# Attention ahead of a soft mixture of experts: softmax weights as the stationary operand, values with a column of ones as the moving one

## The chip, the cores and the metric

The kernel runs on one core of a Trainium2 chip. A core has a matrix engine (TensorE, PE in the profile; its weight loads have a row of their own, PEld), a vector engine (VectorE, DVE), a scalar engine for functions and copies (ScalarE, ACT), a general engine (GpSimd, POOL) and SyncE (SP), which here only issues DMAs. The engines run side by side, each through its own instructions in order, and wait for each other by semaphores. TensorE multiplies a stationary operand, which a weight load brings into its array, by a moving operand that is streamed past it, and writes to PSUM, a small memory of eight banks of 2 KB per partition. ScalarE and VectorE carry results from there to SBUF, the main on-chip memory; GpSimd reads and writes only SBUF.

The metric is the device time of one execution in microseconds (us).

## The reference

```
rotate(x)  = rotary embedding of q and k, by position and frequency       # batch 8, heads 8, seq 576, dim 64
scores     = rotate(q) @ rotate(k).T / sqrt(64)
attn       = exp(scores - max(scores))
attn       = attn / (sum(attn) + 1e-9)
x          = attn @ v                            # joined over heads: 4608 tokens x 512
logits     = x @ phi                             # 4608 x 32 slots
d          = softmax of logits over the tokens;  slot_input = d.T @ x
slot_out   = relu(slot_input[e] @ w1[e]) @ w2[e] # 8 experts, 4 slots each, 512 -> 1024 -> 512
c          = softmax of logits over the slots
out        = c @ slot_out                        # 4608 x 512, float32
```

Everything is float32. Only the score products are split by the kernel into float16 high and low halves.

## The kernel before

The work is cut into 32 pairs of heads (`NPAIR`): two heads of one batch, one on partitions 0 to 63 and the other on 64 to 127. Four pairs make a batch. The 576 tokens are nine blocks of 64 keys, and the queries are two halves of 288 (`HC`). Small products use TensorE's array as four quadrants of 64x64, so that four products of 64 rows and 64 columns can run at once; an entry such as `64*64 64x288` in the profile is one such product, stationary shape first, moving shape second. A float32 product takes two rows in the profile, a float16 product one.

For each pair, by the names in the code:

- `load0`, `load1` (L137) bring q and k; `spin0`, `spin1` (L142, GpSimd) multiply by cosines and sines, `join` (L146, VectorE) adds the two products, `high0`, `high1` (L151, ScalarE) and `low` (L155, VectorE) split the result into float16 halves. The loaded tile `x_in` has two buffers, and `low` is its last reader. `load_v` (L161) brings the values.
- `m00` to `m31` and `m_rem` (L175, L183) are score products of the high halves alone, and VectorE takes their maximum per query (L177, L185); `m_min`, `m_turn`, `m_half`, `m_rows` (L193, L200, L204, L209) make rows of it, which a small DMA puts into `peak`.
- `t0` to `t8` (`score`, L225) are the scores of one key block with **keys on partitions** and queries along the free axis: three float16 products and a fourth that subtracts the maxima, 16 rows in all. ScalarE takes the exponential (L226) into `a_t`, three key blocks to a buffer, three buffers.
- `av0` to `av8` (L238): the values of a key block (64 keys x 64) are stationary and the softmax weights (64 keys x 288 queries) are moving. The result `o_ps` has the value's 64 dimensions on partitions, that is, x transposed and not yet divided. There is one `o_ps`, of two banks. `o_out` (L246, ScalarE) copies it to `xt`.
- The softmax's sums are made apart: `add` (L252, VectorE) adds three key blocks to three others, `total` (L263, TensorE) multiplies by columns of ones (`pick`) so that the sums of both heads come out as rows, `total_out` (L269) copies them. `send` (L274), `recip` (L280), `spread` (L286) and `widen` (L293) carry the sums through SBUF and DRAM and back as a full tile of reciprocals by DMAs; `norm` (L297, GpSimd) multiplies `xt` by it. The last two pairs do this by products instead (`sums_turn`, `sums_wide`, `norm_wide`: L303, L317, L322).
- `natural` (L331, L332) turns the divided `xt` back by transposes of 128x128, and `natural_out` (L337, L338, ScalarE) copies it to `xn`, tokens on partitions. `logits` (L346) needs `xt`, once per batch for four pairs; the slot products of the batch (L389 to L404) need `xn`; they are done in small steps (`step0` to `step2`), with the softmax over slots (L411 to L427).

Score, maximum, sums, turning and logits products share three PSUM tiles of two banks (`ps_s`), taken in turn.

The order of each engine's instructions is written by hand. `WHEN` gives every step an offset; four units of offset are one pair, and step `s` of pair `p` stands at `WHEN[s] + 4p`. All engines' instructions, the DMA issues on SyncE among them, are issued in that order.

The experts' weights are loaded during attention into free SBUF (`weights`, `trickle0` to `trickle3`) as far as it holds them. After the last pair come a tail for that pair and the last batch (L674 to L780), the experts (L789, L813) and the combination with output DMAs (L840 to L843). In the tail `swap` (L685) and `keep` (L679) are products whose results nobody reads. `swap` uses float32 products of 64x64 stationary by 64x65 moving in the four quadrants.

```
for n in range(2):                                   # av, L235 to L239
    for h in range(2):
        r = rows[h ^ n]
        nc.tensor.matmul(o[rows[h], n, 0:HC], lhsT=vt[r, i, n], rhs=ats[p, g][r, b, half[n]],
                         start=(i == 0), stop=(i == NB - 1))
```

## Time and profile before

| | |
|---|---|
| median of 3 runs | 550.15 us (550.13 to 553.4) |
| the profiled execution's own time | 549.75 us |
| its span in the profile | 548.0 us |
| attention, first to last `o_out` (L246) | 46.3 to 473.6 us |
| busy: PE, PEld, DVE, ACT, POOL | 515.7, 389.2, 429.7, 311.6, 326.4 us |
| moved by DMAs | 111.35 MB, mean 203 GB/s |

The profile is one execution. A row of a group reads: line, engine, operation, output<-inputs, shapes, xcount, then busy time in us and mean duration of one in ns, then the idle time of the engine just before them and what ended it. A row of the timeline reads: start in us, length in us, engine, line, operation, xcount. A row of the table by stretches reads: stretch, its length, busy time and number of instructions of PE, PEld, DVE, ACT and POOL, granted TensorE clock (1.00 is full), share of the DMA engines' time, GB/s. Matmuls are pipelined, so several overlap and a row's length holds the latency of its last one.

### The profile page before, as it was taken

The page shows a single profiled execution, that of the slowest core. Times are in us where ns is not written, and L with a number is a line of the kernel's source. Part 1 is how long each engine was busy: PE and PEld are TensorE (multiplying, and loading weights), DVE is VectorE, ACT ScalarE, POOL GpSimd, SP SyncE. Part 2 cuts the span into 40 slices and gives each one's busy share as a digit, 9 for nine tenths or more (in the row PEclk, how much of TensorE's full clock was granted, in tenths as well). Part 3 has the DMA queues.
Part 4 walks back from the last instruction along what each step waited for, and adds up shares of the span by engine and source line. Part 5 has one row for each costly group of instructions (what it writes and reads, how often), then busy time and mean ns, then how long its engine had stood idle before and what let it go on. Part 6 is the DMA issues. An engine that isn't in the chain of part 4 may idle for free.

```text
span 548.0 us, 25344 instructions
## 1 busy us (share of the span) xinstructions
PE 515.7 (94%) x11325; PEld 389.2 (71%) x11325; DVE 429.7 (78%) x580; ACT 311.6 (57%) x655; POOL 326.4 (60%) x324
## 2 busy tenths in 40 slices
PE   4679999999999999999999999999999999999982
PEld 2267787877787777777887788777878886754551
DVE  5779998879998999899988998899889953232352
ACT  2146566666666666656675666566656665354441
POOL 1957787666886688668876887687678111210000
PEclk9689999999999999999999999999999999999997
DMA  7264566666566566556655665566434256459998
GB/s 263 93 216 134 193 194 193 193 192 193 194 194 193 192 192 195 190 183 202 196 195 159 220 197 195 169 204 206 138 120 121 70 182 218 169 190 411 407 417 343
DMA packets 51292, 111.35 MB, mean 203 GB/s; under 512 B 11504, under 2 KB 28656, under 8 KB 51184
## 3 DMA queue, kind: packets, MB, share of 16 engines
q1 hardware_dynamic: 51170, 109.73, 59.7%
q8 instruction: 89, 1.46, 1.1%
q14 instruction: 19, 0.16, 0.1%
q10 hardware_dynamic: 14, 0.00, 0.0%
HBM read 99.93 MB, written 9.58 MB: 200 GB/s over the span
## 4 chain that ended last, share of the span: by engine, by line
PE 87%; DVE 6%; DMA 4%; ACT 1%; issue 1%; SPq 0%; DVEq 0%; ACTq 0%
PE o_ps L238 26%; PE s_ps L225 26%; PE s_ps L263 9%; PE s_ps L175 6%; PE s_ps L331 3%; PE s_ps L789 3%; PE s_ps L346 2%; DVE nm L177 2%; DMA w_exp<-in_w 2%; PE s_ps L400 1%; PE s_ps L813 1%; PE s_ps L200 1%; DVE x_in L146 1%; DMA out<-w_exp 1%; PE s_ps L183 1%; DMA x_in<-in_qk 1%
## 5 line engine op out<-in xcount | busy, mean ns | idle before, releaser
L142 POOL TENSOR_TENSOR x_in<-x_in,cs_sb 128x288 f32<-128x288 f32 x248 | 254.5, 1063 | 80.8 <-DMA x_in<-in_qk 69.0
L226 ACT ACTIVATE a_t<-s_ps 128x576 f32<-128x576 f32 x288 | 179.6, 653 | 89.5 <-PE s_ps L225 89.2
L177 DVE TENSOR_REDUCE nm<-s_ps 128x2 f32<-128x576 f32 x256 | 183.0, 750 | 41.3 <-PE s_ps L175 39.5
L238 PE MATMUL o_ps<-a_t,v_in 64*64 64x288 f32 x2304 | 195.8, 408 | 0.0
L225 PE MATMUL s_ps<-hl 64*64 64x288 f16 x3456 | 166.5, 285 | 4.1 <-DVE nm L177 3.2
L225 PEld LDWEIGHTS <-hl 64*64 64x64 f16 x3456 | 124.6, 107 | 29.4 <-issue 6.5
L225 PE MATMUL s_ps<-peak,lift 64*64 64x288 f16 x1152 | 99.8, 284 | 0.3 <-issue 0.3
L238 PEld LDWEIGHTS o_ps<-a_t,v_in 64*64 64x64 f32 x2304 | 85.7, 133 | 8.2 <-issue 0.5
L175 PE MATMUL s_ps<-hl 64*64 64x288 f16 x1024 | 79.6, 290 | 4.1 <-DVE nm L177 4.0
L297 POOL TENSOR_TENSOR xt<-xt,rb 128x576 f32<-128x576 f32 x30 | 48.0, 1599 | 32.2 <-ACT a_t L226 13.1
L252 DVE TENSOR_TENSOR c_t<-a_t 128x1728 f32<-128x1728 f32 x32 | 62.8, 1961 | 0.0
L155 DVE TENSOR_TENSOR hl<-x_in,hl 128x1152 f16<-128x1152 f32 x32 | 60.1, 1880 | 0.5 <-ACT hl L151 0.5
L175 PEld LDWEIGHTS <-hl 64*64 64x64 f16 x1024 | 38.3, 106 | 24.7 <-issue 15.5
L146 DVE TENSOR_TENSOR x_in<-x_in 128x1152 f32<-128x1152 f32 (+2 forms) x36 | 55.3, 1535 | 0.1
L151 ACT CAST hl<-x_in 128x576 f16<-128x576 f32 (+1 forms) x66 | 40.1, 653 | 23.5 <-DVE x_in L146 21.6
L225 PEld LDWEIGHTS <-lift 64*64 64x64 f16 x1152 | 46.5, 107 | 0.7 <-issue 0.5
L337 ACT COPY xn<-s_ps 128x512 f32<-128x512 f32 x31 | 18.1, 583 | 29.1 <-PE s_ps L332 29.1
L420 POOL TENSOR_TENSOR ln<-ln,cm 128x160 f32<-128x160 f32 x7 | 14.7, 2096 | 32.4 <-DVE cm L419 32.4
L269 ACT ACTIVATE s<-s_ps,bits 128x144 f32<-128x144 f32 x32 | 12.2, 381 | 34.6 <-ACT xn L338 14.2
L263 PE MATMUL s_ps<-c_t,pick 128*32 128x144 f32 x768 | 30.4, 289 | 0.7 <-DVE c_t L252 0.5
L263 PE MATMUL s_ps<-a_t,pick 128*32 128x144 f32 x768 | 29.7, 286 | 0.0
L263 PEld LDWEIGHTS s_ps<-c_t,pick 128*32 128x32 f32 x768 | 21.1, 109 | 6.3 <-issue 4.7
(175 smaller groups left out, 463.7 us busy)
## 6 DMA issues: line engine op xcount, KB each, us to landing
x_in<-in_qk SPq DMA_DIRECT2D x62, 576.0 KB
w_exp<-in_w SPq DMA_DIRECT2D x63, 512.0 KB
v_in<-in_v SPq DMA_DIRECT2D x32, 576.0 KB
out<-w_exp SPq DMA_DIRECT2D x18, 512.0 KB
rb<-r_row SPq DMA_DIRECT2D x60, 144.0 KB
x_in<-in_qk SPq DMA_DIRECT2D x4, 288.0 KB
cs_sb<-in_cs SPq DMA_DIRECT2D x2, 288.0 KB
wk<-in_w SPq DMA_DIRECT2D x1, 512.0 KB
```

What stands on the lines that cost most here:

```text
L142: eng.tensor_tensor(out=x[:, :, c], in0=x[:, :, c], in1=cs_sb[:, :, c], op=ALU.mult)
L146: nc.vector.tensor_tensor(out=x[:, t, 0, c], in0=x[:, t, 0, c], in1=x[:, t, 1, c], op=ALU.add)
L151: nc.scalar.copy(out=halves[p][:, 1 + t, c], in_=loaded[p][:, t, 0, c])
L155: nc.vector.tensor_tensor(out=hl[:, 0:4:3], in0=x[:, :, 0], in1=hl[:, 1:3], op=ALU.subtract)
L175: nc.tensor.matmul(s[rows[c ^ h], h, 0:HC], lhsT=hl[rows[h], QH, at:at + 64], rhs=hl[rows[h], KH, half[n]], start=True, stop=True)
L177: nc.vector.tensor_reduce(out=nms[p][:, n, j:8:4], in_=s[:, :, 0:HC], axis=AX.X, op=ALU.max, negate=True)
L225: nc.tensor.matmul(s[rows[h ^ n], n, 0:HC], lhsT=lhs, rhs=rhs, start=(x == 0), stop=(x == 3))
L226: nc.scalar.activation(out=ats[p, g][:, b].rearrange("p (n x) -> p n x", n=2), in_=s[:, :, 0:HC], func=AF.Exp, scale=SCALE)
L238: nc.tensor.matmul(o[rows[h], n, 0:HC], lhsT=vt[r, i, n], rhs=ats[p, g][r, b, half[n]], start=(i == 0), stop=(i == NB - 1))
L252: nc.vector.tensor_tensor(out=c, in0=ats[p, 0], in1=ats[p, 1], op=ALU.add)
L263: nc.tensor.matmul(s[32 * k:32 * k + 32, 0, 0:QC], lhsT=pick[:, 16 * n:16 * n + NS], rhs=(c, a)[x // GRP][:, x % GRP, QC * k:QC * k + QC], ...
L297: eng.tensor_tensor(out=xts[p], in0=xts[p], in1=rbs.pop(p), op=ALU.mult)
```

## The change

The product of softmax weights and values is turned round. A block of 64 keys x 64 queries of the softmax weights is now stationary, and the values of the key block (64 keys x 65) are moving. The 65th column of the values is all ones, appended on the host before the launch, so column 65 of the result is the sum of the softmax weights of each query. Queries come out on partitions. For each key block and pair there are 5 query blocks x 2 halves x 2 heads = 20 products; the fifth query block of each half overlaps its neighbour by 32 queries, since 288 is not a multiple of 64.

With that:

- `add`, `total`, `total_out`, `send`, `spread`, `widen`, `sums_turn`, `sums_wide`, `norm_wide` and their tiles go.
- `o_out` copies 2 x 325 columns to `o_sb`, and a small piece (32 partitions) to its place. `recip` (VectorE) adds 1e-9 to ten sums per partition and takes the reciprocal; `norm` (GpSimd) multiplies by it, broadcast along 64 columns, and writes `xn` directly.
- `natural` makes `xt` from `xn`, in the other direction than before, by 18 float32 products of 64x64 with the identity, and `natural_out` copies it to `xt`.
- For the last pair `norm_last` does the division on VectorE straight from PSUM; the tail's dummy products are `keep` alone.
- `a_t` holds one key block, with five buffers, in place of three blocks and three buffers. `v_in` moves to another pool; `xn` gets a second buffer.
- All offsets in `WHEN` are new. The written start-up order becomes the table `EARLY`, with the same steps in the same order. All events of all pairs are sorted once.
- The order of output rows changes with the order of queries; the host puts them back.

```diff
-N_A = 3
+N_A = 5
 WHEN = {
...
-    -1.617, "m_half": -1.613, "m_rows": -0.965, "t0": -0.022, "weights": 0.144, "t1": 0.412, "t3": 0.469,
-    "trickle0": 0.55, "av0": 0.559, "t4": 0.734, "t5": 0.974, "t2": 1.021, "step0": 1.301, "av1": 1.367, "av3":
...
-    "trickle3": 3.55, "av6": 3.726, "send": 3.739, "av8": 4.36, "o_out": 4.366, "sums_turn": 4.847,
...
+    "load0": -14.043, "load1": -13.839, "spin0": -12.647, "spin1": -10.775, "join": -8.82, "high0": -7.86,
+    "high1": -7.28, "low": -6.571, "m01": -6.082, "m10": -5.808, "m00": -5.219, "m11": -4.394, "m21": -3.683,
+    "m20": -3.282, "m30": -3.213, "m31": -2.371, "m_rem": -1.686, "m_min": -1.251, "m_turn": -1.007, "m_half":
+    -0.955, "load_v": -0.217, "weights": 0.144, "m_rows": 0.478, "t0": 0.478, "trickle0": 0.55, "t3": 0.846,
+    "t1": 1.021, "t2": 1.273, "av0": 1.383, "t5": 1.452, "t4": 1.466, "trickle1": 1.55, "step0": 1.561, "av3":
+    1.773, "av1": 1.875, "t6": 2.093, "av4": 2.24, "t7": 2.32, "trickle2": 2.55, "t8": 2.695, "step2": 2.733,
+    "av2": 2.893, "av5": 3.27, "step1": 3.28, "av6": 3.379, "trickle3": 3.55, "av7": 4.077, "av8": 4.747,
+    "o_out": 4.753, "recip": 5.468, "norm": 6.011, "natural": 7.348, "natural_out": 7.577, "logits_late": 7.868,
+    "logits": 8.028, "logits_out": 8.396, "stats": 8.996, "logits_out_late": 9.497,
 }
...
     def load_v(p):
-        vts[p] = late.tile([P, NB, 2, 64], F32, name="v_in")
+        vts[p] = att.tile([P, NB, 2, 65], F32, name="v_in", bufs=2)
...
     def score(p, i):
-        g, b = divmod(i, GRP)
-        if b == 0:
-            ats[p, g] = att.tile([P, GRP, S], F32, name="a_t", bufs=N_A)
+        ats[p, i] = att.tile([P, S], F32, name="a_t", bufs=N_A)
...
     def av(p, i):
...
-        o, vt, (g, b) = os_[p], vts[p], divmod(i, GRP)
-        for n in range(2):
-            for h in range(2):
-                r = rows[h ^ n]
-                nc.tensor.matmul(o[rows[h], n, 0:HC], lhsT=vt[r, i, n], rhs=ats[p, g][r, b, half[n]],
-                                 start=(i == 0), stop=(i == NB - 1))
+        o, vt, at = os_[p], vts[p], ats.pop((p, i))
+        for u in range(5):
+            for n in range(2):
+                for h in range(2):
+                    r, q = rows[h ^ n], (HC * n + 64 * u if u < 4 else (256, 512)[n])
+                    nc.tensor.matmul(o[rows[n], h, 65 * u:65 * u + 65], lhsT=at[r, q:q + 64], rhs=vt[r, i, n],
+                                     start=(i == 0 and u == 0), stop=(i == NB - 1 and u == 4))
...
     def o_out(p):
-        xts[p] = late.tile([P, S], F32, name="xt", bufs=N_X)
-        nc.scalar.copy(out=xts[p].rearrange("p (n x) -> p n x", n=2), in_=os_.pop(p)[:, :, 0:HC])
...
+        osb[p] = t = att.tile([P, 2, 5, 65], F32, name="o_sb", bufs=N_O)
+        o = os_.pop(p)
+        nc.scalar.copy(out=t.rearrange("p h u x -> p h (u x)"), in_=o[:, :, 0:325])
+        nc.scalar.copy(out=t[32:64, :, 4, :], in_=o[96:128, :, 260:325])
+
+    def recip(p, src=None):
+        src = osb[p] if src is None else src
+        rrs[p] = rr = small.tile([P, 2, 5], F32, name="rr", bufs=2)
+        nc.vector.tensor_scalar_add(out=rr, in0=src[:, :, :, 64], scalar1=1e-9)
+        nc.vector.reciprocal(out=rr, in_=rr)
 
     def norm(p, eng):
-        eng.tensor_tensor(out=xts[p], in0=xts[p], in1=rbs.pop(p), op=ALU.mult)
...
+        eng.tensor_tensor(out=xn[:, :, 0:4], in0=t[:, :, 0:4, 0:64],
+                          in1=rr[:, :, 0:4].unsqueeze(3).broadcast_to([P, 2, 4, 64]), op=ALU.mult)
+        eng.tensor_tensor(out=xn[0:64, :, 4], in0=t[0:64, :, 4, 0:64],
+                          in1=rr[0:64, :, 4].unsqueeze(2).broadcast_to([64, 2, 64]), op=ALU.mult)
...
     def natural(p):
...
-        for j in range(4):
-            nc.tensor.transpose(t[:, 0, j * P:(j + 1) * P], xt[:, j * P:(j + 1) * P], id_sb)
-        nc.tensor.transpose(t[0:64, 1, 0:P], xt[:, 512:576], id_sb)
...
+        for j in range(5):
+            for r in range(2 if j < 4 else 1):
+                for c in range(2):
+                    nc.tensor.matmul(t[rows[c], r, 64 * j:64 * j + 64],
+                                     lhsT=xns[b][rows[r], j, pp * P + 64 * c:pp * P + 64 * c + 64],
+                                     rhs=id_sb[rows[r], rows[r]], start=True, stop=True)
+
+    def natural_out(p, copy=nc.scalar.copy, rest=nc.scalar.copy):
+        xts[p] = xt = late.tile([P, S], F32, name="xt", bufs=N_X)
+        t = flat.pop(("n", p))
+        copy(out=xt[:, 0:512].rearrange("p (j r x) -> p j r x", j=4, r=2),
+             in_=t[:, :, 0:256].rearrange("p r (j x) -> p j r x", j=4))
+        rest(out=xt[:, 512:S], in_=t[:, 0, 256:320])
...
-    swap(6, 64)
-    sums_turn(p)
-    swap(3, 64)
-    sums_wide(p)
-    norm_wide(p)
-    swap(6, 32)
+    norm_last(p)
+    keep(9)
+    natural(p)
+    natural_out(p, rest=nc.vector.tensor_copy)
+    keep(5)
     logits(p)
     logits_out(p, True)
-    natural(p)
-    swap(8, 64)
+    keep(9)
...
+    vl = np.concatenate([vl, np.ones_like(vl[..., :1])], axis=-1)
```

More of the change, by code (lines that the diff above doesn't have):

```diff
@@ L611, in attn_softmoe @@
             high(0, t, c)
[L612 to L616 removed]
+    done.update((n, 0) for n in ("spin0", "spin1", "join", "high0", "high1", "load0", "load1"))
+    done.add(("join", 1))
+    cold = bank2()
     heat(N_WARM)
[L619 to L622 removed]
```

250 lines of the change are left out of this document (70 added, 180 removed), and 6 rows, old and new, of tables (EARLY, WHEN).

## The prediction

> **What bounds the kernel now.** I read the page first, for the engines and the chain that ended last, then the table by stretches and the list of waits, for whether that engine ever waits in the steady stretch.
>
> ```profile
> PE 515.7 (94%) x11325; PEld 389.2 (71%) x11325; DVE 429.7 (78%) x580; ACT 311.6 (57%) x655; POOL 326.4 (60%) x324
> PE 87%; DVE 6%; DMA 4%; ACT 1%; issue 1%; SPq 0%; DVEq 0%; ACTq 0%
> 180.00:220.00 40.00, 40.00 (x964) 31.64 (x957) 37.90 (x47) 25.38 (x52) 30.74 (x29) 1.00 0.62 196
> PE s_ps L225 <- issue: 1.1, 2, 0.8
> 98.72 0.64 ACT L246 COPY xt<-o_ps 128x576 f32<-128x576 f32 x1
> 430.86 0.64 ACT L246 COPY xt<-o_ps 128x576 f32<-128x576 f32 x1
> ```
>
> TensorE (PE) carries 87% of the chain. In the stretch from 180 to 220 us it is busy for all of its 40.00 us at full clock (1.00), VectorE (DVE) for 37.90. The fourth line is all that the list of waits has for PE between 60 and 440 us. So an attention pair (two heads) costs what PE needs for it, with DVE close behind. L246 runs once per pair; between its fifth and its twenty-ninth run lie 24 pairs, so one takes (430.86 - 98.72) / 24 = 13.84 us.
>
> A busy share says little about one kind of matmul, because four 64x64 quadrants overlap. I therefore take the distance from the start of one row to the start of the next, in one steady pair:
>
> ```profile
> 204.29 0.30 PE L175 MATMUL s_ps<-hl 64*64 64x288 f16 x4
> 204.53 0.66 PE L331 MATMUL s_ps<-id_sb,xt 128*128 128x128 f32 x4
> 205.02 0.27 PE L332 MATMUL s_ps<-id_sb,xt 128*64 128x128 f32 x1
> 205.22 0.94 PE L263 MATMUL s_ps<-c_t,pick 128*32 128x144 f32 x24
> 205.98 0.92 PE L263 MATMUL s_ps<-a_t,pick 128*32 128x144 f32 x24
> 206.83 0.32 PE L175 MATMUL s_ps<-hl 64*64 64x288 f16 x4
> ...
> 208.11 0.32 PE L225 MATMUL s_ps<-peak,lift 64*64 64x288 f16 x4
> 208.23 0.32 PE L175 MATMUL s_ps<-hl 64*64 64x288 f16 x4
> 208.35 0.68 PE L238 MATMUL o_ps<-a_t,v_in 64*64 64x288 f32 x8
> 208.84 0.56 PE L225 MATMUL s_ps<-hl 64*64 64x288 f16 x12
> ```
>
> One `av` unit (L238, 8 rows: four f32 products, two rows each) holds PE for 208.84 - 208.35 = 0.49 us. The sums (L263) hold it for 206.83 - 205.22 = 1.61, the transposes of x (L331, L332) for 205.22 - 204.53 = 0.69. Four rows of L175 take 208.35 - 208.23 = 0.12 among their own kind but 0.24 ahead of L331: changing from 64x64 tiles to 128x128 costs 0.12.
>
> **The av units.** Each becomes 20 products of 64x65, 40 rows with 40 weight loads. The kernel before already holds that shape, by accident of its tail (L685 keeps PE busy there):
>
> ```profile
> L685 PE MATMUL o_ps<-acc,id_sb 64*64 64x65 f32 x136 | 2.7, 222 | 0.8 <-ACT xt L246 0.8
> 475.54 0.58 PE L685 MATMUL o_ps<-acc,id_sb 64*64 64x65 f32 x24
> 476.05 1.22 PE L317 MATMUL s_ps<-id_sb,rn 72*64 72x72 f32 x32
> 479.36 1.16 PE L685 MATMUL o_ps<-acc,id_sb 64*64 64x65 f32 x64
> ```
>
> It has the same stationary size, moving width, quadrants and banks. Taking the last row's length (0.22) from the busy time, a start follows a start by (1.16 - 0.22) / 63 = 15.0 ns; in the burst of 24 by (0.58 - 0.22) / 23 = 15.7. A new unit then takes 40 x 15.0 = 0.60 us, 0.11 more than 0.49; nine units: **+0.99 us per pair**. Bounds: if only columns counted, 61 ns per row x 65/288 = 13.8 ns (0.55 us a unit); if quadrants overlapped no better than the 72x72 products of L317, which run two at a time, (1.22 - 0.22) / 31 = 32 ns (1.28 us). I take 15.0, the row of the same shape.
>
> The Trainium skill, "TensorE: Matmul & The Clock Gate", section "Wait — 56ns, not 53.3ns?", says that starts never come closer than about 25 ns, however few columns; by that a unit would be 1.0 us and the kernel would end near 630. As a distance between starts the burst's 15.0 ns disagrees and leaves it no chance; as a pace kept up for long it is the first rival.
>
> **What PE loses.** `total` goes: **-1.61** (24 products, 48 rows). `natural` becomes 18 products of 64x64, 36 rows: 36 x 15.0 = 0.54 for 0.69, **-0.15**, and stays in 64x64 tiles, **-0.12**. Sum per pair: +0.99 - 1.61 - 0.15 - 0.12 = **-0.89 us**.
>
> **The other engines**, which must follow at 13.84 - 0.89 = 12.95 us:
>
> ```profile
> L177 DVE TENSOR_REDUCE nm<-s_ps 128x2 f32<-128x576 f32 x256 | 183.0, 750 | 41.3 <-PE s_ps L175 39.5
> L252 DVE TENSOR_TENSOR c_t<-a_t 128x1728 f32<-128x1728 f32 x32 | 62.8, 1961 | 0.0
> L155 DVE TENSOR_TENSOR hl<-x_in,hl 128x1152 f16<-128x1152 f32 x32 | 60.1, 1880 | 0.5 <-ACT hl L151 0.5
> L146 DVE TENSOR_TENSOR x_in<-x_in 128x1152 f32<-128x1152 f32 x30 | 51.1, 1705 | 0.0
> L280 DVE RECIPROCAL rr<-rc 96x12 f32<-96x12 f32 x30 | 6.4, 213 | 0.0
> L142 POOL TENSOR_TENSOR x_in<-x_in,cs_sb 128x288 f32<-128x288 f32 x248 | 254.5, 1063 | 80.8 <-DMA x_in<-in_qk 69.0
> L297 POOL TENSOR_TENSOR xt<-xt,rb 128x576 f32<-128x576 f32 x30 | 48.0, 1599 | 32.2 <-ACT a_t L226 13.1
> L427 POOL TENSOR_TENSOR cn_sb<-ln,cm 128x160 f32<-128x160 f32 x7 | 3.2, 459 | 2.6 <-DVE cm L426 2.6
> L226 ACT ACTIVATE a_t<-s_ps 128x576 f32<-128x576 f32 x288 | 179.6, 653 | 89.5 <-PE s_ps L225 89.2
> L269 ACT ACTIVATE s<-s_ps,bits 128x144 f32<-128x144 f32 x32 | 12.2, 381 | 34.6 <-ACT xn L338 14.2
> L338 ACT COPY xn<-s_ps 64x128 f32<-64x128 f32 x31 | 8.0, 258 | 0.0
> ```
>
> DVE needs nine maxima x 0.75 + 1.96 + 1.88 + 1.71 + 0.21 = 12.51 us per pair; without the 1.96 of `c_t` and with one more small operation like L280 (0.21) 10.76, so it falls further behind PE. GpSimd (POOL) multiplies 512 + 128 elements by a broadcast: at L427's 2.87 ns each 1.84 us for 1.60, and 8 x 1.06 + 1.84 = 10.3 is still under 12.95. ScalarE (ACT) copies 650 columns (0.72) and a small piece (0.26) where it copied 576 (0.64, the rows of L246 above), and drops L269 (0.38): nothing gained or lost. All are costed at nothing, because PE's 12.95 us covers them; if DVE or POOL ran short, the price would be what it exceeds that by.
>
> **Queues and buffers.** The offsets of the written order count four to a pair, so one is 3.2 us. SyncE loses `send`, `spread` and `widen` (two issues) per pair, which stood ahead of x_in loads. The maxima's rows go out on SyncE behind `load_v` and a weight load and must land before t0: from `m_half` (-0.955) to t0 (0.478) are 1.43 offsets, 4.6 us.
>
> ```profile
> 204.25 0.25 ACT L204 ACTIVATE mr<-s_ps 9x128 f16<-9x128 f32 x1
> ```
>
> Before, L204 ends at 204.50 and the rows are used at 208.11, so 3.6 us are enough: no cost. `load_v` moves from -3.19 to -0.217 and is used at 1.383 (1.6 offsets, 5.2 us later); x_in, loaded from -14.043 as soon as `low` of two pairs back has freed its buffer, is rotated from -12.647 on (1.4 offsets, 4.5 us). In the pair shown a load of that size is used 4.1 us after its issue, POOL waiting for it:
>
> ```profile
> 212.25 0.33 SPq L137 DMA_DIRECT2D x_in<-in_qk  x1
> ...
> 216.39 8.29 POOL L142 TENSOR_TENSOR x_in<-x_in,cs_sb 128x288 f32<-128x288 f32 x8 [2.15 <-DMA x_in<-in_qk]
> ```
>
> So both are in time, x_in by little; a late one costs POOL first, which has 2.6 us to spare in a pair, and PE only behind that. Nothing.
>
> A softmax buffer now holds one key block, five in all; by the order at most five are open at once (t8 of a pair waits for none that `av` has not freed), again no cost. On ACT `high1` (0.72) and the longer `o_out` (0.753) now stand ahead of the exponentials of t3, t1, t2, while PE may run only three score banks ahead: at 0.65 us per exponential and 0.48 per score unit (16 rows, L175's four being 0.12) PE may stand there for up to 0.5 us a pair. Against it stands DVE's relief, up to 0.3. I take **+0.10 per pair**.
>
> **Ends.** The last two pairs lose the sums by products: L317 above for pair 30 (1.2 us; pair 31's lies in the tail). In the tail:
>
> ```profile
> 473.63 0.64 ACT L246 COPY xt<-o_ps 128x576 f32<-128x576 f32 x1
> 478.20 0.54 PE L346 MATMUL s_ps<-xt,phi_sb 128*32 128x128 f32 x16
> L337 DVE COPY xn<-s_ps 128x512 f32<-128x512 f32 x1 | 0.7, 681 | 0.0
> ```
>
> From the last `av` to the logits 478.20 - 473.63 = 4.6 us. After: two small DVE operations (0.5), a multiply like L337 on DVE (0.68), two small ones (0.26 each, as ACT's L338), `natural` 0.54, its copy 0.6 (as L246's 0.64), handovers 0.5 (estimated): 3.3. Gain 1.3, between 0 and 2; the weight stage behind it only shifts. The start-up I leave as it is.
>
> **Sum.** 31 distances between `o_out`s x (-0.89 + 0.10) = -24.5; -1.2; -1.3: **-27.0 us**. Against the profiled run's 549.75 us (span 548.0): 522.8; the median of the runs shown is 0.4 higher: **523**.
>
> **Rivals.** *PE can't issue so densely for long (slower).* A pair would hold 360 av, 144 score, 36 maxima, 36 `natural` and some 24 other rows: 600, each with its weight load. 12.95 us ask for 21.6 ns per row throughout; the stretch above has 964 in 40 us, 41 ns. The densest long stretch I found:
>
> ```profile
> 474.33:478.33 4.00, 3.90 (x160) 3.50 (x164) 1.01 (x2) 0.30 (x1) 1.26 (x2) 1.00 0.43 135
> ```
>
> It is 25 ns per row, and its first burst came after 0.8 us of idling (L685's row) in which instructions could pile up. For: nothing in the trace shows 21.6 ns kept up. Against: the longer burst is no slower (64 rows at 15.0, 24 at 15.7). It decides from 13.84 / 600 = 23.1 ns; at 25 ns a pair takes 15.0, 31 x 1.16 = +36 - 2.5: **583**. Chance 0.15.
>
> *Waits take the gain (no change).* The stall behind `high1` and `o_out`, with units of 40 loads that each wait for an exponential, costs PE 0.9 us a pair. For: three score banks, one output bank pair, shorter pairs. Against: no such wait now in 380 us, and the order leaves 2.9 us (0.9 offsets) from t0 to av0, in which 1.1 us of t0's own work lie (0.48 + 0.65). A pace of 17.5 ns in the `av` rows would do the same (2.5 x 360 = 0.9). 31 x (-0.89 + 0.90) - 2.5: **547**, chance 0.13.
>
> *More than that (faster).* At 13.8 ns and with DVE's relief a further 0.43 + 0.3 a pair: **500 to 510**, chance 0.05.
>
> Forecast, within 510 to 537 (15.7 ns and 0.3 more waits at the top): 0.67. A comparison here tells 1%, 5.5 us, from no change. Faster: 0.67 + 0.05 and 0.01 of the rival of waits; within 1%: 0.11 of that rival; slower: its last 0.01 + 0.15. The range from 505 to 553 leaves out the slow rival and the ends of the other two, 2 in 10.
>
> **What would show it.** Right: L263, L252, L280 rows gone; 11,520 rows of 64x65 with 0.58 to 0.64 us a unit; 12.7 to 13.4 us between `o_out`s; DVE's share down. Wrong: units above 0.69 us with PE "waiting for nothing" (issue), or PE waits on exponentials or maxima of over 0.5 us a pair.

## The result, and the profile after

The changed kernel takes 744.06 us (median; 740.96 to 752.44), the kernel before 550.14 us beside it. The ratio is 1.349, with a 95% interval from 1.340 to 1.359; it leaves out the run of 752.44 us, which is over 1.5% above the fastest. The forecast was 523 us, with a range from 505 to 553: a gain was forecast, and the kernel became a third slower.

The page of the changed kernel, whose profiled execution took 746.48 us: busy time of the engines, the queue that brings instructions (packets, MB, share), the chain that ended last, and TensorE's groups in attention.

```profile
PE 557.8 (75%) x19764; PEld 468.5 (63%) x19764; DVE 356.2 (48%) x579; ACT 315.3 (42%) x654; POOL 253.6 (34%) x352
...
q8 instruction: 155, 2.54, 1.4%
...
PE 68%; issue 21%; DMA 6%; DVE 3%; ACT 1%; SPq 0%; ACTq 0%; DVEq 0%
...
L235 PE MATMUL o_ps<-v_in,a_t 64*64 64x65 f32 x11520 | 268.4, 231 | 93.9 <-issue 93.4
L235 PEld LDWEIGHTS o_ps<-v_in,a_t 64*64 64x64 f32 x11520 | 243.3, 144 | 108.7 <-issue 103.9
...
L221 PE MATMUL s_ps<-hl 64*64 64x288 f16 x3456 | 186.7, 304 | 38.9 <-issue 38.1
```

No engine is the bound any more. TensorE fell from 94% of the span to 75%, VectorE to 48%, GpSimd to 34%. What grew is "issue", from 1% of the chain to 21%: TensorE stands still and waits for nothing that the profile can name. It does so ahead of the new `av` rows (93.4 us) and ahead of the score rows (38.1 us), which the change left alone. The same queue on the page of the kernel before:

```profile
q8 instruction: 89, 1.46, 1.1%
```

The packets rose by 66 and the data by 1.08 MB. TensorE has 19,764 - 11,325 = 8,439 more products and as many more weight loads, 16,878 instructions; 1.08 MB over these are 64 bytes each. So the queue brings TensorE's program in packets of 16 KB, 256 instructions or 128 rows (a product with its load). I call such a packet a page.

The table by stretches of the changed kernel: the stretch that the prediction read, and two that begin and end where TensorE starts again after standing still.

```profile
180.00:220.00 40.00, 28.98 (x1236) 25.96 (x1228) 20.97 (x33) 18.18 (x38) 15.28 (x22) 0.99 0.34 120
189.43:193.53 4.10, 3.07 (x129) 2.93 (x128) 1.58 (x4) 2.83 (x5) 1.40 (x2) 1.00 0.64 201
193.53:199.45 5.92, 3.00 (x129) 2.56 (x130) 2.27 (x4) 0.65 (x1) 4.96 (x7) 1.00 0.67 256
```

The table counts 129 rows from one restart to the next, both times; the last of them is the row that starts at the end of the stretch and opens the next page. So it is 128 rows, exactly one page. TensorE needs about 3 us for them and gets the next after 4.10 and 5.92 us. Over the 40 us it issues 1,236 rows, one per 32.4 ns, where the same stretch of the kernel before had 964. In TensorE's timeline:

```profile
189.43 0.31 PE L221 MATMUL s_ps<-hl 64*64 64x288 f16 x2 [0.58 <-issue]
...
193.53 0.97 PE L235 MATMUL o_ps<-v_in,a_t 64*64 64x65 f32 x49 [1.03 <-issue]
...
195.02 0.79 PE L235 MATMUL o_ps<-v_in,a_t 64*64 64x65 f32 x39
...
195.97 0.56 PE L221 MATMUL s_ps<-hl 64*64 64x288 f16 x10
199.45 0.31 PE L221 MATMUL s_ps<-hl 64*64 64x288 f16 x2 [2.92 <-issue]
...
203.08 0.50 PE L284 MATMUL s_ps<-id_sb,xn 64*64 64x64 f32 x17 [0.76 <-issue]
```

The stop at 196.53 falls into a score unit, between its tenth and eleventh product, where neither an operand nor the output is new. Inside a page the array is as fast as forecast: 39 `av` rows start within (0.79 - 0.22) us, 15.0 ns apart. The copies of `o_ps` give the pair:

```profile
L245 ACT COPY o_sb<-o_ps x26: 701/704/705, 107.3 to 615.4; 128x650 f32<-128x650 f32 x26
```

(615.4 - 107.3) / 25 = 20.32 us a pair, for 13.84 before and 12.95 forecast. A long stretch of the change, and 24 pairs of the kernel before:

```profile
107.00:600.00 493.00, 371.12 (x14496) 327.63 (x14499) 249.02 (x395) 218.32 (x457) 192.64 (x259) 0.92 0.32 114
```

```profile
98.72:430.86 332.14, 331.78 (x7883) 261.26 (x7876) 301.80 (x391) 211.97 (x452) 244.86 (x229) 1.00 0.58 183
```

Over the long stretch of the change a row comes each 493 / 14,496 = 34.0 ns. A pair thus has about 600 rows, as the prediction counted, or 4.7 pages. TensorE stands still for 121.9 of the 493 us, 5.0 us a pair, and the mean granted clock is 0.92, where it was 1.00 before.

### The profile page after: what moved, and what is told of

Its sections match the earlier page's. It is cut to its first block, busy times and chain, and to the rows that moved or that the text cites. A ratio compares the mean times of both kernels' runs of the same rounds, so it can differ in the third digit from the quotient of the medians.

```text
span 744.7 us, 42027 instructions
## 1 busy us (share of the span) xinstructions
PE 557.8 (75%) x19764; PEld 468.5 (63%) x19764; DVE 356.2 (48%) x579; ACT 315.3 (42%) x654; POOL 253.6 (34%) x352
## 4 chain that ended last, share of the span: by engine, by line
PE 68%; issue 21%; DMA 6%; DVE 3%; ACT 1%; SPq 0%; ACTq 0%; DVEq 0%
PE o_ps L235 28%; PE s_ps L221 23%; PE s_ps L173 5%; DMA w_exp<-in_w 4%; PE s_ps L284 3%; PE s_ps L301 2%; DVE nm L175 2%; PE s_ps L181 1%; PE s_ps L355 1%; PE s_ps L690 1%; PE s_ps L198 1%; DMA out<-w_exp 1%; DMA x_in<-in_qk 1%; DVE x_in L144 0%; PE s_ps L591 0%
## 5 line engine op out<-in xcount | busy, mean ns | idle before, releaser
L235 PE MATMUL o_ps<-v_in,a_t 64*64 64x65 f32 x11520 | 268.4, 231 | 93.9 <-issue 93.4
L235 PEld LDWEIGHTS o_ps<-v_in,a_t 64*64 64x64 f32 x11520 | 243.3, 144 | 108.7 <-issue 103.9
L175 DVE TENSOR_REDUCE nm<-s_ps 128x2 f32<-128x576 f32 x256 | 185.9, 756 | 244.7 <-PE s_ps L173 242.9
L140 POOL TENSOR_TENSOR x_in<-x_in,cs_sb 128x288 f32<-128x288 f32 x248 | 197.1, 831 | 63.0 <-DMA x_in<-in_qk 62.9
L221 PE MATMUL s_ps<-hl 64*64 64x288 f16 x3456 | 186.7, 304 | 38.9 <-issue 38.1
L221 PE MATMUL s_ps<-peak,lift 64*64 64x288 f16 x1152 | 120.4, 303 | 8.6 <-issue 8.6
L262 POOL TENSOR_TENSOR xn<-o_sb,rr 128x512 f32<-128x512 f32 x31 | 32.4, 1046 | 263.1 <-ACT a_t L222 147.2
L173 PE MATMUL s_ps<-hl 64*64 64x288 f16 x1024 | 100.2, 298 | 14.7 <-DVE nm L175 8.8
L173 PEld LDWEIGHTS <-hl 64*64 64x64 f16 x1024 | 49.7, 111 | 23.1 <-issue 22.4
L183 DVE TENSOR_REDUCE nm<-s_ps 128x2 f32<-128x576 f32 x32 | 24.3, 759 | 51.7 <-PE s_ps L181 51.5
L153 DVE TENSOR_TENSOR hl<-x_in,hl 128x1152 f16<-128x1152 f32 x32 | 43.1, 1348 | 0.5 <-ACT hl L149 0.5
L291 ACT COPY xt<-s_ps 128x512 f32<-128x512 f32 x32 | 18.7, 585 | 55.3 <-PE s_ps L284 55.3
L284 PEld LDWEIGHTS s_ps<-id_sb,xn 64*64 64x64 f32 x1152 | 24.3, 147 | 7.8 <-issue 7.8
L284 PE MATMUL s_ps<-id_sb,xn 64*64 64x64 f32 x1152 | 27.3, 232 | 0.8 <-issue 0.8
L245 ACT COPY o_sb<-o_ps 128x650 f32<-128x650 f32 x31 | 21.8, 703 | 8.9 <-PE o_ps L235 4.8
L181 PE MATMUL s_ps<-hl 64*64 64x288 f16 x128 | 19.8, 355 | 6.5 <-issue 5.3
```

Source lines behind the costliest of these rows:

```text
L140: eng.tensor_tensor(out=x[:, :, c], in0=x[:, :, c], in1=cs_sb[:, :, c], op=ALU.mult)
L153: nc.vector.tensor_tensor(out=hl[:, 0:4:3], in0=x[:, :, 0], in1=hl[:, 1:3], op=ALU.subtract)
L173: nc.tensor.matmul(s[rows[c ^ h], h, 0:HC], lhsT=hl[rows[h], QH, at:at + 64], rhs=hl[rows[h], KH, half[n]], start=True, stop=True)
L175: nc.vector.tensor_reduce(out=nms[p][:, n, j:8:4], in_=s[:, :, 0:HC], axis=AX.X, op=ALU.max, negate=True)
L181: nc.tensor.matmul(s[rows[h], n, 0:HC], lhsT=hl[rows[h], QH, 512:S], rhs=hl[rows[h], KH, half[n]], start=True, stop=True)
L221: nc.tensor.matmul(s[rows[h ^ n], n, 0:HC], lhsT=lhs, rhs=rhs, start=(x == 0), stop=(x == 3))
```

## The theories

**Supply.** Pages of TensorE's program come no faster than one in some 3.5 to 4 us, and later when data transfers run; a kernel that uses them up faster waits. **Array.** The new products themselves (65 moving columns, five times as many loads, the exponentials as the loaded operand) take the array longer than the burst of the prediction showed. **Data.** Loads of q, k, v and weights hold up the pages or TensorE. The experiments with few rows removed or added also test whether the time follows the count of rows alone.

## Experiments: the count of rows

**The kernel before, with its `av` products cut into pieces.** Roles, loaded values and number formats stay; only the 288 moving columns are cut, so that the columns in all are the same. Five pieces give exactly the 11,520 `av` rows of the change.

```diff
-        for n in range(2):
-            for h in range(2):
-                r = rows[h ^ n]
-                nc.tensor.matmul(o[rows[h], n, 0:HC], lhsT=vt[r, i, n], rhs=ats[p, g][r, b, half[n]],
...
+        cut = [HC * c // 5 for c in range(5 + 1)]
+        for c in range(5):
+            for n in range(2):
+                for h in range(2):
+                    r = rows[h ^ n]
+                    nc.tensor.matmul(o[rows[h], n, cut[c]:cut[c + 1]], lhsT=vt[r, i, n],
+                                     rhs=ats[p, g][r, b, HC * n + cut[c]:HC * n + cut[c + 1]],
```

> The kernel before with each av product cut into five pieces of 57 or 58 columns: values still stationary, softmax weights still moving, the sums as before, but 40 rows and 40 weight loads a unit, as in the changed kernel. Theory of instruction supply (TensorE gets its instructions in pages of 256, and a page takes some 4.1 us to come): a pair holds some 334 + 288 = 622 rows, 1,244 instructions, 4.9 pages, so 20 us a pair for 13.8 and 730 to 790 us in all, with idle gaps at every 256th instruction. Rival, the operands' roles (a weight load of what ScalarE has just written is slow or waits for it): no such loads here, so the rows only cost their columns, 40 x 14 ns a unit, and the time is 555 to 590 us.

Measured: 763.1 us. Its page has about the same idle time ahead of its `av` rows (94.0 us) as the changed kernel's (93.9):

```profile
PE 591.3 (78%) x20541; PEld 494.2 (65%) x20541; DVE 424.9 (56%) x580; ACT 316.7 (42%) x655; POOL 306.0 (40%) x324
...
q8 instruction: 161, 2.64, 1.4%
...
PE 74%; issue 18%; DMA 3%; DVE 3%; ACT 1%; SPq 0%; ACTq 0%; DVEq 0%
...
L240 PE MATMUL o_ps<-a_t,v_in 64*64 64x58 f32 (+1 forms) x11520 | 254.8, 227 | 94.0 <-issue 93.8
```

So the loss needs no exchange of roles, no column of ones and no new order of work: as many instructions in the old roles are enough for it.

With three pieces:

> The kernel before with each av product cut into three pieces of 96 columns: 24 rows a unit, 334 + 144 = 478 rows a pair. Theory of instruction supply at 32 to 35 ns per row: 15.3 to 16.7 us a pair for 13.84, so 595 to 640 us. Without such a limit: 552 to 562 us.

Measured: 640.84 us, 0.8 us above the window of supply. With two:

> The kernel before with each av product cut into two pieces of 144 columns: 16 rows a unit, 334 + 72 = 406 rows a pair, the array's time nearly unchanged. Theory of instruction supply at 32 to 35 ns per row with data on the DMA engines (changed kernel and the cut into five): 13.0 to 14.2 us a pair for 13.84, so it begins to show: 550 to 575 us. Without such a limit: 550 to 556 us.

Measured: 577.69 us, 2.7 us above the window that I gave to supply, and 22 us above the other. From two pieces to five, 6,912 more rows cost 185.4 us, 26.8 ns each. From none to two, 2,304 rows cost 27.7 us, 12 ns each: there the pages begin to come late. The share of "issue" in the chain agrees: 1% before, 4% with two pieces, 11% with three, 18% with five.

**Nothing but rows.** The kernel before, with 4,096 rows at its end that need nothing and that nobody waits for, half with 65 columns and half with 16:

```diff
+    for w in (65, 16):
+        for i in range(256):
+            for c in range(2):
+                for r in range(2):
+                    at = 65 * (i % 5)
+                    nc.tensor.matmul(dense[rows[c], r ^ c, at:at + w], lhsT=id_sb[rows[r], 64 * c:64 * c + 64],
+                                     rhs=acc[rows[r], at:at + w], start=True, stop=True)
```

> The kernel before with 1,024 more f32 products of 64x64 stationary behind its last product, whose results nobody reads: 1,024 rows with 65 moving columns, then 1,024 rows with 16... in all 2,048 products would be 4,096 rows; here 512 x 4 = 2,048 products, half of them with 65 columns, half with 16, 4,096 rows and 8,192 instructions, 32 pages. No load hides them or runs beside their later part. Theory of instruction supply: after the first pages, which are there, both halves run at one pace, some 3.6 us per 256 instructions, 28 ns per row, whatever their width, and about 115 us are added (640 to 670 us in all). Rival, the array alone: 15 ns per row with 65 columns and less with 16, at most 55 us added (at most 605 us).

Measured: 661.67 us. TensorE's timeline in the half with 65 columns:

```profile
538.48 3.60 PE L907 MATMUL s_ps<-acc,id_sb 64*64 64x65 f32 x229
545.81 5.68 PE L907 MATMUL s_ps<-acc,id_sb 64*64 64x65 f32 x256 [3.73 <-issue]
...
552.75 2.09 PE L907 MATMUL s_ps<-acc,id_sb 64*64 64x65 f32 x128 [1.26 <-issue]
556.22 2.09 PE L907 MATMUL s_ps<-acc,id_sb 64*64 64x65 f32 x128 [1.38 <-issue]
559.97 2.09 PE L907 MATMUL s_ps<-acc,id_sb 64*64 64x65 f32 x128 [1.65 <-issue]
563.71 2.09 PE L907 MATMUL s_ps<-acc,id_sb 64*64 64x65 f32 x128 [1.65 <-issue]
567.73 2.09 PE L907 MATMUL s_ps<-acc,id_sb 64*64 64x65 f32 x128 [1.93 <-issue]
```

This is supply in its pure form. The half begins with 229 rows without a stop, more than one page: before it TensorE used its program slowly, and more than a page was there. After that a page of 128 rows is issued in one go, (2.09 - 0.22) / 127 = 14.7 ns a row, and then TensorE stands until the next. Pages start 3.47, 3.75, 3.74 and 4.02 us apart: 27 to 31 ns a row. (The group at 545.81 is two pages; the first of them ran at a granted clock of 0.55 and ended only when the next was there.) The table by stretches, once for 20 us of this half and once for 20 us of the half with 16 columns:

```profile
550.00:570.00 20.00, 11.96 (x744) 11.13 (x736) 0.00 (x0) 0.00 (x0) 0.00 (x0) 1.00 0.02 5
600.00:620.00 20.00, 18.57 (x676) 18.35 (x680) 0.00 (x0) 0.00 (x0) 0.00 (x0) 0.52 0.02 4
```

The first needs 20 / 744 = 26.9 ns a row with the DMA engines 2% busy. The second says nothing of supply, because the granted clock is 0.52 there, and 14.7 ns at that clock would be 28. The moved data in 40 slices of half a microsecond, from 540 to 560 us:

```profile
GB/s 410 401 410 410 426 426 410 418 393 369 197 172 147 98 0 0 0 0 0 0 33 0 0 0 0 0 0 33 0 0 0 0 0 0 33 0 0 0 0 0
```

The three slices of 33 GB/s are one page each (33 x 0.5 us = 16 KB), seven slices apart. So the transfer takes a seventh of the time between pages or less. Each of the three is over more than 2 us before the next page starts (552.75, 556.22 and 559.97). What the rest of the time is, the trace doesn't show.

The Trainium skill, "Runtime: NRT & Kernel Launch", section "Instruction fetch mechanics", gives blocks of 16 KB and 256 instructions as well, but calls the cost of crossing one "mostly hidden". Here it is not hidden from a kernel that wants a row more often than each 27 to 31 ns, and with data transfers beside it the loss begins earlier.

## Experiments: array and data

**Twice the columns.** In eight of nine units the change's products take both heads' values, 130 columns for 65. That changes the result, as the text on record says.

```diff
-                    nc.tensor.matmul(o[rows[n], h, 65 * u:65 * u + 65], lhsT=at[r, q:q + 64], rhs=vt[r, i, n],
+                    if i == 0:
+                        dst, rhs = slice(65 * u, 65 * u + 65), vt[r, i, n]
+                    else:
+                        dst = slice(65 * min(u, 3), 65 * min(u, 3) + 130)
+                        rhs = vt[r, i].rearrange("p n x -> p (n x)")
+                    nc.tensor.matmul(o[rows[n], h, dst], lhsT=at[r, q:q + 64], rhs=rhs,
```

> The changed kernel with twice the moving columns in eight of nine av units (the values of both heads, 130 columns, added up in the same places, so that x is no longer attention): the same instructions, twice the array's time in them. Theory of instruction supply: a page of av takes the array 3.6 us at most, no more than it takes to come, so the time stays: 735 to 775 us. Rival, the array's own time (65 columns in four quadrants cost more than the burst showed): 8 x 40 x 13 ns = 4.2 us more a pair, 860 to 890 us.

Measured: 749.14 us, 5 us from the changed kernel. In the stretch from 180 to 220 us:

```profile
180.00:220.00 40.00, 35.90 (x1228) 33.20 (x1218) 22.07 (x33) 18.15 (x38) 15.58 (x22) 1.00 0.33 120
```

TensorE is busy for 35.90 us where the change has 28.98, and issues the same rows, 1,228 for 1,236. The added array time fell into the idle time. Array, as the bound of the changed kernel, is out for this stretch, where the clock is the same (1.00 for 0.99). Over all of attention the mean clock is 0.97 here for 0.92 in the change, so the equal times of the whole runs may hide two differences that offset each other.

**Fewer data transfers.** The change, with q and k loaded in full for the first four pairs only, and values for two; later pairs reuse old data and load a quarter.

```diff
-        nc.sync.dma_start(out=loaded[p][:, t], in_=qk[p, t])
+        c = full if p < 4 else slice(0, HC // 2)
+        nc.sync.dma_start(out=loaded[p][:, t, :, c], in_=qk[p, t][:, :, c])
...
-        vts[p] = att.tile([P, NB, 2, 65], F32, name="v_in", bufs=2)
-        nc.sync.dma_start(out=vts[p], in_=v[p])
+        if p < 2:
+            vts[p] = att.tile([P, NB, 2, 65], F32, name="v_in", bufs=2)
+            nc.sync.dma_start(out=vts[p], in_=v[p])
+        else:
+            vts[p] = vts[p - 2]
```

> The changed kernel with fewer data DMAs during attention: the values are loaded for the first two pairs only and used again, and of q and k only a quarter of the columns is loaded from the fifth pair on (the rotation is written aside; x is no longer attention). 0.8 MB a pair for 2.3. Theory of instruction supply with a page that waits behind data on the DMA engines: pages come in some 3.7 us for 4.14 on average, a pair takes 18.1 us for 20.3, 660 to 700 us. If the page's time does not depend on the data: 735 to 755 us. Rival of the operands' roles: unchanged as well.

Measured: 689.45 us, 55 us less than the change; without most of the data transfers 139 us of the loss are left. The stretch from 107 to 600 us again:

```profile
107.00:600.00 493.00, 388.01 (x16121) 341.58 (x16112) 270.37 (x429) 239.37 (x505) 215.70 (x268) 0.98 0.16 49
```

A pair takes 18.3 us here (`o_out` from 119.8 to 595.6 us in 26 distances), 2.0 less than in the change. Of these, 1.1 are shorter stops (3.9 us a pair for 5.0), as the page of 5.92 us above lets one expect (DMA engines 67% busy). The other 0.9 are a shorter busy time, and it goes with a granted clock of 0.98 for 0.92. What moves the clock, no run shows.

**A smaller part, both ways.** The change with `natural` as five whole transposes in place of 18 products (5 rows for 36 a pair):

```diff
-        for j in range(5):
-            for r in range(2 if j < 4 else 1):
-                for c in range(2):
-                    nc.tensor.matmul(t[rows[c], r, 64 * j:64 * j + 64],
...
+        for j in range(4):
+            nc.tensor.transpose(t[:, 0, j * P:(j + 1) * P], xn[:, j], id_sb)
+        nc.tensor.transpose(t[:, 1, 0:64], xn[0:64, 4], id_sb[0:64, 0:64])
```

> The changed kernel with natural by five transposes of 128x128 (five rows) in place of 18 products of 64x64 (36 rows); the result is the same. It costs the array 0.15 us more a pair and two changes of tile mode. Theory of instruction supply: 31 rows less at 33 ns are 1.0 us a pair, so 705 to 720 us. Without such a limit: 0.3 us a pair more, 750 us.

Measured: 728.97 us, 15 us less where supply said 24 to 39, so 9 us above its window. Of the 992 rows saved each gave 15 ns, not 27; why, no run shows. The reverse, that `natural` in 64x64 products alone in the kernel before:

```diff
-        for j in range(4):
-            nc.tensor.transpose(t[:, 0, j * P:(j + 1) * P], xt[:, j * P:(j + 1) * P], id_sb)
...
+        for j in range(5):
+            for c in range(2 if j < 4 else 1):
+                for r in range(2):
+                    at = j * P + 64 * c
+                    nc.tensor.matmul(t[rows[c], r, 64 * j:64 * j + 64], lhsT=xt[rows[r], at:at + 64],
```

> One part of the change alone: the kernel before with its natural by 18 products of 64x64 with the identity (36 rows for 5), all else as before. Theory of instruction supply: 334 + 31 = 365 rows a pair at 33 ns are 12.0 us, below the 13.84 that the array needs, so the part is worth what the prediction said of it without the change of mode, 0.15 us a pair less: 543 to 549 us. If pages already come late at times in the kernel before: up to 1% slower, 550 to 556 us.

Measured: 557.25 us, ratio 1.0132 (1.0102 to 1.0162). The prediction had put 0.27 us a pair to this part's credit. It costs 1.3%, a little more than the window for pages that come late at times. The kernel before already uses a page in 5.3 us (964 rows in 40 us), so supply is the likely reason, but no run shows it.

## Experiments: is the exchange of roles worth anything?

If rows are the price, the same exchange with few rows should gain. These kernels take 128 keys to a contraction and 128 queries to a load, so that both halves of the partitions hold keys of one head: 50 products, 100 rows a pair for 360. `natural` goes by whole transposes.

```diff
-        for u in range(5):
-            for n in range(2):
-                for h in range(2):
-                    r, q = rows[h ^ n], (HC * n + 64 * u if u < 4 else (256, 512)[n])
-                    nc.tensor.matmul(o[rows[n], h, 65 * u:65 * u + 65], lhsT=at[r, q:q + 64], rhs=vt[r, i, n],
...
+        for j in ((0, 1), (2, 3, 4))[m] if i < 8 else range(5):
+            n = int(j >= 2)
+            q, w = 128 * j - 256 * n, (128 if j < 4 else 64)
+            for h in range(2):
+                if i < 8:
+                    lhs, rhs = at[:, h, q:q + w], vt[:, 2 * kb + h]
...
+                nc.tensor.matmul(o[0:w, h, 65 * j:65 * j + 65], lhsT=lhs, rhs=rhs, start=not opened[p][h],
```

With the units in clusters, so that TensorE changes tiling less often:

> The same exchange of roles as in the change (the exponentials are loaded, the values with their column of ones move, queries on partitions, sums in column 65), but with 128 keys to a contraction and 128 queries to a load: a pair's weighted sums take 100 rows instead of 360, the turn to natural order takes five whole transposes, and all nine units of a pair are issued in four clusters. Nothing of the computation is left out. A pair then holds some 310 rows, fewer than before the change (334). Supply theory: nothing waits for pages of the program, gaps in TensorE's records with all inputs there stay under 10 us in the span, and the time is 525 to 565 us (the array has 100 rows at about 60 ns, 6.0 us a pair, where the kernel before has 9 units of 0.49 us, 4.4 us). Rival (what costs is the exchange itself: 65 moving columns, loads of exponentials, sums by a column of ones): most of the 194 us stays, over 640 us.

Measured: 737.81 us (736.4 to 738.22), ratio 1.342 (1.338 to 1.346). With the units in between, as in the change:

> As the kernel with clusters, but each unit of weighted sums stands between score units as in the change, so that TensorE goes between 64-row and 128-row tiles some 18 times a pair instead of 8. Supply theory: 535 to 585 us, 5 to 25 us above the clustered one, at 0.1 us or so to a change of tiling, with the same few gaps at pages. Rival (the exchange itself costs): over 640 us.

Measured: 734.91 us (734.77 to 737.37), ratio 1.337 (1.333 to 1.341). Both miss the windows of supply: the times are those that the rival expected, and the added changes of tiling cost nothing that can be seen. But the profile of the clustered one is not that of the change:

```profile
PE 691.5 (94%) x10452; PEld 567.4 (77%) x10452; DVE 359.1 (49%) x642; ACT 306.4 (42%) x686; POOL 253.9 (35%) x352
...
PE 86%; ACT 5%; DVE 3%; issue 3%; DMA 2%; SPq 0%; DVEq 0%; ACTq 0%
...
L252 PE MATMUL o_ps<-v_in,a_t 128*128 128x65 f32 (+3 forms) x3200 | 354.8, 271 | 0.0
```

There are fewer rows than in the kernel before, issue is 3%, and TensorE is busy 94%: the array, not supply. 3,200 `av` rows hold it for 354.8 us, 111 ns each on average over four shapes. I had reckoned 60, four times the quadrants' 15 ns.

**The price of one such row by itself.** The kernel before with whole-array products at its end, a new load for each:

```diff
+    for k, w in ((id_sb, 65), (id_sb, 16), (id_sb, 130), (lift, 65)):
+        for i in range(256):
+            at = 130 * (i // 2 % 3)
+            rhs = acc[:, at:at + w] if k is id_sb else peaks[0][:, at:at + w]
+            nc.tensor.matmul(dense[:, i % 2, at:at + w], lhsT=k, rhs=rhs, start=True, stop=True)
```

> The kernel before with four stretches of whole-array products at its end, a new 128 by 128 load for each: 256 products of 32 bits with 65 columns, 256 with 16, 256 with 130 (two rows each), and 256 of 16 bits with 65 columns. Load-and-product-in-turn theory: 116 ns a row with 65 columns, at least 70 with 16 (the load alone), 160 to 180 with 130, so that the columns explain the smaller part. Rival (the load hides behind the product before it, as the four quadrants' do): the pace follows the columns: under 40 ns with 16, which is then the pace of supply, near 29, and 110 with 130. The time in all: 548 + 120 to 210 us.

Measured: 771.03 us in all. Four stretches, in the order 65, 16, 130 columns of 32 bits, and 65 of 16 bits:

```profile
571.00:581.00 10.00, 10.00 (x92) 10.00 (x91) 0.00 (x0) 0.00 (x0) 0.00 (x0) 1.00 0.01 2
620.00:640.00 20.00, 20.00 (x96) 20.00 (x95) 0.00 (x0) 0.00 (x0) 0.00 (x0) 0.50 0.00 1
734.00:744.00 10.00, 10.00 (x92) 10.00 (x91) 0.00 (x0) 0.00 (x0) 0.00 (x0) 1.00 0.01 2
761.00:765.00 4.00, 4.00 (x139) 4.00 (x136) 0.00 (x0) 0.00 (x0) 0.00 (x0) 1.00 0.02 4
```

A row takes 10 / 92 = 109 ns with 65 columns and with 130, and 208 ns with 16 at half the clock, which would be 104 at the full one. Neither theory is right: the load sets the pace, and the product hides behind it, up to 130 columns at least. The Trainium skill, "TensorE: Matmul & The Clock Gate", section "LDWEIGHTS (loading the stationary operand)", makes a load columns / 1.2 ns; for 128 columns an estimate by it is 107 ns, and this trace agrees for 32 bits. With 16 bits a row comes each 4 / 139 = 28.8 ns, so such a load takes no more than that. The pace is in the range of supply's, but the rows come evenly and TensorE is busy for all of the 4.00 us, without the stops of the dense stretch; whether the load or supply sets it, the run doesn't show.

This explains most of the clustered kernel's time. 13.84 us without `av` (9 x 0.49 = 4.4) and `total` (1.61), with 100 rows of 109 ns (10.9), is 18.7 us a pair; it is an estimate, since a fifth of these rows load 64 columns only. Its `o_out`s:

```profile
L265 ACT COPY o_sb<-o_ps x5: 593/593/594, 207.3 to 286.8; 128x520 f32<-128x520 f32 x5
```

They lie (286.8 - 207.3) / 4 = 19.9 us apart; of the other 1.2 us nothing was tried. That it ends near the changed kernel's time is a coincidence of two prices: 100 loads at 109 ns, or 600 rows at 34 ns.

**16 bits in the changed kernel.** One load and one row for each product instead of two, all else as in the change:

```diff
-        ats[p, i] = att.tile([P, S], F32, name="a_t", bufs=N_A)
+        ats[p, i] = att.tile([P, S], F16, name="a_t", bufs=N_A)
...
+    def cast_v(p):
+        v32, vts[p] = vts[p], att.tile([P, NB, 2, 65], F16, name="v_half", bufs=2)
+        nc.vector.tensor_copy(out=vts[p], in_=v32)
```

> The changed kernel with one part of the computation changed: the exponentials and the values are rounded to 16 bits (one more VectorE cast a pair for the values), so that a product takes one load and one row where 32 bits take two. Roles, tiles, the column of ones and the order of work stay. A pair's weighted sums take 180 rows instead of 360, the whole pair some 420 instead of 600, nearly those of the two-piece cut of the kernel before (406 rows, 577.7 us). Supply theory: 545 to 600 us, gaps at every 256 instructions but short. Rival (65 moving columns and loads of exponentials cost as such, whatever the count): over 650 us.

Measured: 583.88 us (582.11 to 588.72), ratio 1.064 (1.058 to 1.070).

```profile
PE 448.1 (77%) x14004; PEld 346.0 (59%) x14004; DVE 376.5 (65%) x611; ACT 309.6 (53%) x654; POOL 278.1 (48%) x352
...
PE 40%; ACT 20%; issue 17%; DMA 10%; DVE 10%; SPq 1%; ACTq 0%; POOL 0%; DVEq 0%
```

5,760 rows fewer give 160 us back, 27.8 ns each, nearly the slope between the pieces of the first experiment (26.8). Issue is still 17% of its chain. The kernel that keeps the exchange, its order and its tiles lies where its count of rows puts it. (The table leaves out the kernels with fewer transfers or more columns, and those with 128 keys, which the array bounds.)

| kernel | rows on TensorE | us |
|---|---|---|
| before | 11,325 | 550.1 |
| before, `natural` in 64x64 products | 12,317 | 557.3 |
| before, `av` in 2 pieces | 13,629 | 577.7 |
| change, 16 bits | 14,004 | 583.9 |
| before, `av` in 3 pieces | 15,933 | 640.8 |
| change, whole transposes | 18,772 | 729.0 |
| change | 19,764 | 744.1 |
| before, `av` in 5 pieces | 20,541 | 763.1 |

**16 bits with 128 keys.** The clustered kernel with the same two edits:

> The kernel with 128 keys to a contraction, in clusters, with exponentials and values rounded to 16 bits (a part of the computation changed): 50 rows a pair of one pass each instead of 100. In that kernel TensorE was busy 94% of the span, nothing waited at pages, and a row of a whole 128 by 128 load and 65 columns took 116 ns from start to start. If what bounds it is the load and the product of one tile in turn, halving the rows takes at least 50 x 116 ns = 5.8 us off a pair's 19.8, for 540 to 585 us (under 540 if a 16-bit load is shorter too). If the bound of near 735 us that three kernels share is something else (waits between score, exponentials and sums), it stays over 680 us.

Measured: 511.23 us (510.19 to 513.95), ratio 0.932 (0.928 to 0.936): below the window, as the expectation allows in brackets (under 540) when the load gets shorter too. It beats both kernels. But it changes two things, and the kernel before can have 16 bits as well (its values are cast on VectorE in the same way):

```diff
-    pick = const.tile([P, NS + 16], F32, name="pick")
+    pick = const.tile([P, NS + 16], F16, name="pick")
...
-            ats[p, g] = att.tile([P, GRP, S], F32, name="a_t", bufs=N_A)
+            ats[p, g] = att.tile([P, GRP, S], F16, name="a_t", bufs=N_A)
...
-        cts[p] = c = att.tile([P, GRP, S], F32, name="c_t")
+        cts[p] = c = att.tile([P, GRP, S], F16, name="c_t")
```

> The kernel before with exponentials, their sums over groups, the ones that pick rows and the values rounded to 16 bits (a part of the computation changed, as in the 16-bit kernel with 128 keys, 511.2 us): roles as before, values loaded, exponentials moving, column sums by products with ones. Tells whether that kernel's gain comes from the exchange of roles or from 16 bits. If from 16 bits: the weighted sums take 36 rows a pair instead of 72 and the column sums 24 instead of 48, which have 195.8 and 60.1 us of TensorE's records in the kernel before; half of them is at most 128 us, and with the other engines next behind, 450 to 530 us, at or under 511. If the exchange is what gives it: 535 to 555 us.

Measured: 501.72 us (498.89 to 503.42), ratio 0.910 (0.906 to 0.914). So 16 bits are enough for the gain, and the old roles get no less of it. The first row is the chain of this kernel, the second that of the one with 128 keys:

```profile
DVE 47%; PE 31%; DMA 8%; ACT 8%; issue 4%; SPq 1%; ACTq 0%; DVEq 0%
```

```profile
PE 46%; DVE 22%; DMA 18%; issue 6%; ACT 4%; SPq 1%; ACTq 0%; DVEq 0%
```

With the old roles VectorE now has the largest share of the chain; with the new ones, which relieve VectorE, it is still TensorE. The order of work in both is one written for other durations, so the last 10 us between them say little.

## Why the prediction was wrong, by its own steps

**The step that failed** is the one from a burst to a pace: "I take 15.0, the row of the same shape", and with it a pair of 12.95 us that is TensorE's array time alone, though the prediction saw that this asks for "21.6 ns per row throughout". Rows came at 34.0 ns on average, and a pair took 20.32 us.

**The time of the array: nearly right.** "A new unit then takes 40 x 15.0 = 0.60 us": inside a page the rows lie 15.0 ns apart in the change and 14.7 in the dense stretch. The sums are gone, and so are `add`'s 62.8 us on VectorE. The two pages of the result section, at full clock, kept TensorE busy for some 3.0 us each, so 4.7 of them are 14.2 us a pair. About 0.2 us at each page's end lie in that, in which the last row only drains (0.9), so some 13.2 of work for the 12.95 forecast. That error alone would have left a gain. The rest of the 20.32 us, by the long stretch: 5.0 us of standing still, and a busy time of 15.3 us, 1.1 above the 14.2, that goes with the mean clock of 0.92. All but the 5.0 and the 20.32 are estimates from these rows.

**The other engines, queues, buffers and waits: nothing late.** From the changed kernel's list of TensorE's waits between 60 and 620 us (us in total, times, longest):

```profile
PE o_ps L235 <- issue: 78.1, 55, 4.5
PE s_ps L221 <- issue: 42.9, 23, 4.3
...
PE s_ps L173 <- DVE nm L175: 1.7, 2, 0.9
...
PE s_ps L198 <- ACT a_t L222: 0.9, 1, 0.9
```

Waits for other engines come to a few microseconds in all. The rival "Waits take the gain" did not happen. The ends were near the forecast too: from the last `av` row to the logits TensorE takes 3.0 us (671.88 to 674.89) for the 3.3 forecast, of which no row shows the 0.5 of handovers by itself, and from there to the end it is 69.8 us in both kernels. Only the first `o_out` comes 4.1 us later (50.4 for 46.3), which the prediction put at nothing.

**The rival "PE can't issue so densely for long": this is what happened**, with its mechanism, its count of rows (600 forecast, about 600 found) and its point of decision (23.1 ns). Two things in it failed. Its price, 25 ns a row, came from "the densest long stretch I found", four microseconds, and the 160 rows in it are little more than one page. Supply, with the clock that goes with it, gives a row per 34.0 ns here. At that pace the rival's own sum is 600 x 34.0 = 20.4 us a pair, 31 x 6.56 - 2.5 = +201, 751 us, in place of 583. And its chance, 0.15, rested on "the longer burst is no slower (64 rows at 15.0, 24 at 15.7)". A burst of 64 rows is half a page. It shows the pace inside a page and can show nothing of the pace of pages.

**What the forecast lacked is a second resource in the sum.** All terms were time on the array, and the term for 36 `natural` rows in place of 5 was even a gain (-0.27). With supply in the sum, the change goes from some 330 rows a pair to 600, from a page in 5.3 us, which the kernel before just gets (the part with `natural` alone already cost 1.3%), to a page in 12.95 x 128 / 600 = 2.8 us by the forecast, which nothing here ever showed.

**The rule of 25 ns between starts**, which the prediction weighed (the Trainium skill, "TensorE: Matmul & The Clock Gate", section "Wait — 56ns, not 53.3ns?"), does not hold here as a distance between starts (14.7 ns over 128 rows in the dense stretch), yet "near 630" was nearer than the forecast: a floor on rows was the right idea with another cause and size.

## What to carry to other kernels

Count TensorE's instructions of a change beside their array time, products and loads, two of each for a 32-bit product, and compare the count per microsecond with what the trace has kept up over several pages of 256 instructions; a burst shorter than a page proves nothing. When roles are exchanged, also price the loads at their own pace: 128 columns of 32 bits took 109 ns here whatever moved past them. If a new form gains only with another number format, give the old form that format before crediting the new one.
